# Attention and a routed expert layer on one core: the order of the loads at the start of the kernel

## The chip, the core and the metric

The kernel runs on one core of one Trainium2 chip. The metric is the device time of one execution in microseconds (us); less is better. TensorE multiplies matrices and transposes, VectorE (DVE) and ScalarE (ACT) work on rows, GpSimd (POOL) does some of the element work and the indirect transfers, and SyncE (SP) issues nearly all other transfers. Every engine runs its own instructions in order, so an instruction that waits holds back all that stand behind it on its engine; this goes for SP's transfers too.

## What is computed

Causal attention over a window of 128 positions with a slope per head, and then a layer of 8 experts, of which each token takes the one with the largest gate logit:

```
batch, n_heads, seq, head_dim = (8, 8, 576, 64)
scores = scale * np.matmul(q, k.transpose(0, 1, 3, 2))
bias = slopes[:, None, None] * (-np.abs(rel).astype(np.float32))[None, :, :]
mask = (rel >= 0) & (rel < window)
scores = np.where(mask, scores + bias[None], -1000000000.0)
attn = np.exp(scores - max) / (sum + 1e-09);  x = attn @ v
logits = x @ w_gate;  expert_idx = np.argmax(logits, axis=1)
out[token] = gate_w[token] * np.maximum(x[token] @ w1[e], 0.0) @ w2[e]
```

All inputs are float32.

## The kernel before

**Attention** goes over the 8 batches in pairs. 576 rows of a batch are 4 blocks of 128 queries and a rest of 64, and the rests of two batches make one block together, so there are 36 chunks of 128 query rows (`make_chunks`); chunk 4 is the first such pair of rests (batches 0 and 1), chunk 5 the first block of batch 1. A chunk looks at no more than 256 keys: chunk m of a batch needs the key columns from 128(m-1) to 128(m+1). The 8 heads lie in 4 pairs, and a pair fills the 128 partitions with twice 64 values.

A chunk's work is cut into operations with letters, once for each half of the heads where there is a digit: S (bias matmuls from a table, then query times key), F (fold the window and take the row maximum on DVE), E (exponentials on ACT), T (transposes on TensorE), C (copy to `pT` on ACT), P (masks on POOL), A (probabilities times values), X (copy on ACT), R (matmul with `iw_sb`, which holds an identity and the gate weights), L and Y (scaling on DVE, then the write of the rows to DRAM by SP).

**What sets the order.** Attention is recorded in steps (`step(s)`), four to a chunk, and within `tc.manual_schedule` the instructions of every engine stand in just that order up to step 152. The table `WHEN` gives each operation its time in chunks after the chunk's start: S0 of chunk c stands in step 4c, F1 at 0.604, A0 at 2.75 (so A of chunk 0 in step 11, A of chunk 1 in step 15), R at 4.027 (R of chunk 0 in step 16). Loads stand in steps too: `ahead` puts a query block at QA = -16 steps, its scaling on POOL at ZA = -6 and the values at VA = +1 step from the chunk's start.

**The start.** Ahead of step 0 stand, on SP: the first 128 key columns of batch 0 (L62), the table `cb_sb` with the bias in two halves of columns (L117; the first half serves the first two pairs of heads), the masks `c1_sb` (L118), then query block 1, key columns 128 to 320, the constants `c2_sb` (L425; its first 128 columns are the identity of the transposes), query block 2, key columns 320 to 576, value block 0 (L80), `iw_sb` (L133) and value block 1. Query block 0 is issued by ACT. Meanwhile TensorE does 8 matmuls on zeros (L104 and L98) and DVE scales query block 0 (L75). The loads that follow (query blocks 3 and the two rests, the keys of batch 1 by pairs of heads at L67) come out of `ahead` at step 0 and later. Transfers take eight semaphores in turn, so each one waits until the eighth before it has landed.

The weights of the experts' narrow tiles (`w_n`, 1 MB, L847) belong to the later part of the kernel and aren't in the manual order: a scheduler puts each of their loads at a free place on SP.

**The experts** follow: tokens are gathered by expert, and two layers of matmuls with weights split in a high and a low part fill TensorE to the end.

Of the kernel before, what the change touches and what calls it, by code (L numbers as in the profile page):

```python
# [10 lines left out]
F32 = mybir.dt.float32  # L11
# [4 lines left out]
ALU = mybir.AluOpType  # L16
# [16 lines left out]
def keep(tc, ins):  # L33
    return ins if HELD[0] else tc.keep_in_program_order(ins)


def attention(ctx, tc, st, qT, kT, v, c1, cb, iw, load_c2, logits, chunk_done, chunks, begun):
    nc = tc.nc
    const = ctx.enter_context(tc.tile_pool(name="a_const", bufs=1))
    qkv = ctx.enter_context(tc.tile_pool(name="a_qkv", bufs=2))  # L40
# [10 lines left out]
    batch = {}  # L51
    blocks = {}
# [3 lines left out]
        turns.append(turns.pop(0))  # L56
        return turns[-1]

    def load_k(c, d):
        if c == 0:  # L60
            batch[0] = qkv.tile([128, NP, S], F32, name="k_sb", bufs=2)
        nc.sync.dma_start(out=batch[0][:, :, c:d], in_=kT[0][:, :, c:d])  # L62

    def load_pair(b, p):
        if p == 0:
            batch[b] = qkv.tile([128, NP, S], F32, name="k_sb", bufs=2)
        nc.sync.dma_start(out=batch[b][:, p], in_=kT[b][:, p])  # L67

    def load_q(b, m, eng=nc.sync):
        blocks["q", b, m] = q = qkv.tile([128, NP, 128], F32, name="q_sb", bufs=QBUF)  # L70
        eng.dma_start(out=q, in_=qT[b, m])

    def scale_q(eng, b, m):
        q = blocks["q", b, m][:, :, 0:128 if m < 4 else S - 512]
        eng.tensor_scalar(out=q, in0=q, scalar1=0.125, scalar2=1.0, op0=ALU.mult, op1=ALU.mult)  # L75

    def load_v(b, m):
        n = min(128, S - 128 * m)
        blocks["v", b, m] = x = qkv.tile([128, DM], F32, name="v_sb", bufs=VBUF)
        nc.sync.dma_start(out=x[0:n], in_=v[b, 128 * m:128 * m + n])  # L80
# [6 lines left out]
    iw_sb = const.tile([128, NP, XW], F32, name="iw_sb")  # L87
# [23 lines left out]
        bank = score_banks()[:, 0] if op not in "zog" else None  # L111
        st["early"][0](op, bank if bank is None else bank.rearrange("p a b -> p (a b)"))

    load_k(0, 128)
    load_q(0, 0, nc.scalar)
    for c, d in ((0, 576), (576, cb.shape[1])):
        nc.sync.dma_start(out=cb_sb[:, c:d], in_=cb[:, c:d])  # L117
    nc.sync.dma_start(out=c1_sb, in_=c1)  # L118
    first = const.tile([128, 1], F32, name="first")
    nc.vector.memset(first, 0.0)  # L120
# [2 lines left out]
    warm_up(WU[0] - 4)  # L123
    st["warm"] = lambda k: (list(map(early, LE[k])), warm_up(LW[k]))

    scale_q(nc.vector, 0, 0)
    load_q(0, 1)
    load_k(128, 320)
    load_c2()
    load_q(0, 2)  # L130
    load_k(320, S)
    load_v(0, 0)
    nc.sync.dma_start(out=iw_sb, in_=iw)  # L133
    load_v(0, 1)

    def is_tail(subs):
        return subs[0][0] != subs[2][0]
# [95 lines left out]
            in1=rinv.rearrange("q (p c) -> q p c", c=2).unsqueeze(3).to_broadcast([128, NP, 2, n]), op=ALU.mult)  # L233

    ahead = {}
    seen = {("q", 0, 0), ("q", 0, 1), ("q", 0, 2), ("v", 0, 0), ("v", 0, 1), ("z", 0, 0)}
    first = {0}
    for ch, subs in enumerate(chunks):
        for b, m in dict.fromkeys((b, i // 4) for b, i in subs):
            want = [("q", b, m, load_q, QA), ("z", b, m, lambda b, m: scale_q(nc.gpsimd, b, m), ZA),  # L240
                    ("v", b, m, load_v, VA)]
            if m == 4:
                want.append(("v", b, 3, load_v, VA))
            for kind, b, j, f, at in want:
                if (kind, b, j) not in seen:
                    seen.add((kind, b, j))
                    ahead.setdefault(max(0, 4 * ch + at + SHIFT.get((kind, b % 2, j), 0)), []).append((f, b, j))
        for b in {b for b, _ in subs} - first:
            first.add(b)
            for p in range(NP):  # L250
                ahead.setdefault(4 * ch + KA + KD * p, []).append((load_pair, b, p))
    plan = []
    for ch, subs in enumerate(chunks):
        at = {**WHEN[None], **WHEN.get(ch, {})}
# [49 lines left out]
    def step(s):  # L304
        st["step"] = s
        if s == 0:
            begun(0)
        if s == 12:
            begun(1)
        for f, b, m in ahead.get(s, ()):  # L310
            f(b, m)
        while plan and plan[0][0] < (s + 1) / 4 - 1e-6:
            _, _, op, ch = plan.pop(0)
            do(op, ch)
        if s < len(WU) - 1:
# [24 lines left out]
    s = HAND  # L340
# [77 lines left out]
def load_consts(tc, st, c2):  # L418
    nc = tc.nc
    c2_sb = st["r_const"].tile(list(c2.shape), F32, name="c2_sb")  # L420
    o = 0
    for n, w in CONSTS:
        st[n] = c2_sb[:, o:o + w]
        o += w
    return lambda: nc.sync.dma_start(out=c2_sb, in_=c2)  # L425


def moe_setup(ctx, tc, st):
# [16 lines left out]
    st["base"] = base  # L445
    st["idx"] = const.tile([128, E * TT], U32, name="idx")

# [588 lines left out]

def layouts(q, k, v):
    heads = lambda a: a.reshape(B, NP, 2, S, D).transpose(0, 2, 4, 1, 3).reshape(B, 128, NP, S)
    qp = np.zeros((B, 128, NP, 640), q.dtype)
    qp[..., 0:S] = heads(q)  # L1040
    qT = np.ascontiguousarray(qp.reshape(B, 128, NP, 5, 128).transpose(0, 3, 1, 2, 4))
# [11 lines left out]
    return dict(qT=qT, kT=np.ascontiguousarray(heads(k)), v=vv, c1=c1,  # L1053
                cb=cb.reshape(128, -1).astype(ml_dtypes.bfloat16))


# [136 lines left out]


@with_exitstack
def attn_moe_kernel(ctx, tc, qT, kT, v, c1, cb, c2, iw, w12, out):
    nc = tc.nc
    st = {"stages": []}
    moe_pools(ctx, tc, st)
    load_c2 = load_consts(tc, st, c2)  # L1200
    moe_early(ctx, tc, st)
    weight_stream(ctx, tc, st, w12)
    chunks = make_chunks()
    lgs = {}

    with ExitStack() as actx:
# [46 lines left out]
        attention(actx, tc, st, qT, kT, v, c1, cb, iw, load_c2, logits, done, chunks, begun)  # L1253
# [45 lines left out]
```

## Time and profile before

| | us |
|---|---|
| median of 3 runs | 646.49 (645.24 to 649.17) |
| the profiled execution's own time | 648.7 |
| its span in the trace | 646.6 |
| TensorE busy in the span | 632.9 (98%) |
| granted TensorE clock, mean | 0.996 of full |

The profile is of one execution. The span begins 2.1 us or so after what the time counts; a time inside the trace is us from the span's start. A busy share is an average over the whole: what the start costs is read from the first 30 us, in the chain of waits (which piece of work released the next), in the timeline of each engine, and in tables of busy time by stretch, which also give the clock that TensorE was granted.

### The profile page before, as it was taken

What the parts mean: (1) busy time and instruction counts of PE and PEld (TensorE: products, weight loads), DVE (VectorE), ACT (ScalarE), POOL (GpSimd) and SP (SyncE); (2) the same over time, 40 slices, a digit from 0 to 9 for tenths busy, and PEclk for the clock granted to TensorE, in tenths of its full rate; (3) what the DMA queues carried; (4) which work ended last, traced back from release to release, by engine and by line L of the source; (5) the groups of instructions that cost most, each with busy time, mean ns of one, the idle gap of its engine ahead of it and who ended that gap; (6) DMA issues with size and microseconds to landing.
All of it is one profiled execution on the core that took longest, in us unless ns stands there. A gap on an engine that the chain in (4) does not pass through costs nothing.

```text
span 646.6 us, 17910 instructions
## 1 busy us (share of the span) xinstructions
PE 632.9 (98%) x7125; PEld 540.0 (84%) x7125; DVE 382.4 (59%) x940; ACT 318.2 (49%) x963; POOL 294.8 (46%) x405
## 2 busy tenths in 40 slices
PE   7999999999999999999999999999999999999996
PEld 3788888878887988988989899898898888888884
DVE  3458878869888786545543654555455456355411
ACT  5778888889877314533342334334233333333311
POOL 2644648668645040076227606733760750570202
PEclk9899999999999999999999999999999999999999
DMA  8765888777734152473535325434543532544101
GB/s 287 249 204 155 267 262 236 233 255 221 220 105 117 51 172 77 161 251 105 188 109 172 107 75 180 120 90 130 154 108 97 176 120 77 180 118 134 66 1 61
DMA packets 47288, 98.49 MB, mean 152 GB/s; under 512 B 12053, under 2 KB 14101, under 8 KB 47202
## 3 DMA queue, kind: packets, MB, share of 16 engines
q1 hardware_dynamic: 38722, 77.30, 37.8%
q0 software_dynamic: 8336, 19.76, 10.5%
q8 instruction: 57, 0.93, 0.6%
q10 hardware_dynamic: 144, 0.26, 0.1%
q14 instruction: 29, 0.24, 0.1%
HBM read 78.32 MB, written 18.98 MB: 150 GB/s over the span
## 4 chain that ended last, share of the span: by engine, by line
PE 74%; issue 10%; DVE 7%; POOL 4%; ACT 3%; DMA 1%; POOLq 0%; SPq 0%; ACTq 0%; DVEq 0%
PE y_ps L898 25%; PE l_ps L702 24%; PE b_ps L218 7%; PE s_ps L160 5%; PE b_ps L187 4%; PE r_ps L226 4%; POOL xg L682 2%; PE s_ps L151 2%; ACT pe L179 2%; DVE nmax L173 2%; DVE s_ps L170 1%; POOL out L886 1%; PE x_ps L663 1%; DMA cb_sb<-cb 1%; PE y_ps L858 1%
## 5 line engine op out<-in xcount | busy, mean ns | idle before, releaser
L705 ACT ACTIVATE hh<-l_ps 128x336 fp32r<-128x336 f32 (+7 forms) x104 | 46.5, 448 | 203.6 <-PE l_ps L702 203.3
L709 DVE SCALAR_TENSOR_TENSOR hl<-l_ps,hh 128x336 fp32r<-128x336 f32 (+7 forms) x104 | 52.0, 501 | 151.0 <-ACT hh L705 150.8
L682 POOL DMA_INDIRECT xg<-xd,od_idx x112 | 116.5, 1040 | 34.8 <-issue 33.8
L179 ACT ACTIVATE pe<-s_ps,nmax 128x128 f32<-128x128 f32 x288 | 105.5, 383 | 31.5 <-DVE nmax L173 24.7
L898 PE MATMUL y_ps<-wh,hh 128*128 128x512 f32 (+5 forms) x280 | 110.8, 396 | 0.0
L898 PE MATMUL y_ps<-wh,hl 128*128 128x512 f32 (+5 forms) x280 | 110.4, 394 | 0.0
L898 PE MATMUL y_ps<-wl,hh 128*128 128x512 f32 (+5 forms) x280 | 110.2, 394 | 0.0
L886 POOL DMA_INDIRECT out<-y,od_pidx x33 | 34.8, 1056 | 151.7 <-ACT y L904 145.5
L202 POOL TENSOR_SCALAR_AFFINE_SELECT pT<-pT 128x512 f32<-128x512 f32 x112 | 72.1, 652 | 66.4 <-ACT pT L282 65.0
L990 DVE TENSOR_TENSOR wl<-w_raw,wh 128x512 fp32r<-128x512 f32 x114 | 73.9, 690 | 32.0 <-ACT wh L986 30.6
L702 PE MATMUL l_ps<-xh,wh 128*128 128x304 f32 (+9 forms) x416 | 81.7, 318 | 0.0
L702 PE MATMUL l_ps<-xh,wl 128*128 128x304 f32 (+9 forms) x416 | 81.0, 316 | 0.0
L702 PE MATMUL l_ps<-xl,wh 128*128 128x304 f32 (+9 forms) x416 | 80.8, 316 | 0.0
L702 PEld LDWEIGHTS l_ps<-xh,wh 128*128 128x128 f32 x416 | 68.0, 189 | 8.4 <-issue 1.2
L702 PEld LDWEIGHTS l_ps<-xh,wl 128*128 128x128 f32 x416 | 66.3, 189 | 1.9
L702 PEld LDWEIGHTS l_ps<-xl,wh 128*128 128x128 f32 x416 | 66.3, 189 | 1.7
L218 PE MATMUL b_ps<-pT,v_sb 128*64 128x128 f32 (+2 forms) x1152 | 66.1, 265 | 0.1
L218 PEld LDWEIGHTS b_ps<-pT,v_sb 128*64 128x64 f32 (+1 forms) x1152 | 57.0, 136 | 9.3 <-issue 5.1
L898 PEld LDWEIGHTS y_ps<-wh,hl 128*128 128x128 f32 (+5 forms) x280 | 51.4, 183 | 13.6
L179 ACT ACTIVATION_READ_ACCUMULATOR pe<-s_ps,nmax 128x1 f32 x288 | 62.6, 218 | 0.0
L986 ACT CAST wh<-w_raw 128x1024 fp32r<-128x1024 f32 x57 | 59.5, 1044 | 4.6 <-DMA w_raw<-w 4.6
L898 PEld LDWEIGHTS y_ps<-wl,hh 128*128 128x128 f32 (+5 forms) x280 | 51.5, 184 | 11.4
(214 smaller groups left out, 923.1 us busy)
## 6 DMA issues: line engine op xcount, KB each, us to landing
w_raw<-w SPq DMA_DIRECT2D x64, 512.0 KB, 3.7
q_sb<-qT SPq DMA_DIRECT2D x39, 256.0 KB, 4.8
xd<-x_sb SPq DMA_DIRECT2D x32, 258.0 KB, 3.4
v_sb<-v SPq DMA_DIRECT2D x32, 256.0 KB, 4.2
k_sb<-kT SPq DMA_DIRECT2D x28, 288.0 KB, 4.8
w_n<-w SPq DMA_DIRECT2D x4, 1024.0 KB, 5.6
xg<-xd,od_idx POOLq DMA_INDIRECT x112, 3.2
xd<-x_sb SPq DMA_DIRECT2D x8, 129.0 KB, 2.7
```

What stands on the lines that cost most here:

```text
L160: nc.tensor.matmul(out=s_ps[rows(u), c, n, x0:x1], lhsT=blocks["q", b, m][h, 2 * g + n, rows(u % 2 if tail else u)], rhs=batch[b][h, 2 * g ...
L179: nc.scalar.activation(out=pe[:, h, :], in_=s_ps[:, c, n, lo:lo + 128], func=AF.Exp, bias=nmax[:, 2 * c + n:2 * c + n + 1], scale=1.0, acc ...
L202: nc.gpsimd.affine_select(out=part(cut(kb)), in_=part(cut(1)), pattern=pat(sign), base=0, channel_multiplier=-sign, compare_op=op, fill=0.0)
L218: nc.tensor.matmul(out=x_ps[64 * c:64 * c + 64, p, q], lhsT=blocks["v", b, m - 1 + kb][0:kk, D * h:D * h + D], rhs=pT[0:kk, kb, h, q], sta ...
L682: ins = tc.nc.gpsimd.indirect_dma_start(out=g[:, s], out_offset=None, in_=parts, in_offset=bass.IndirectOffsetOnAxis(ap=idx[:, s], axis=0),)
L702: nc.tensor.matmul(out=ps, lhsT=a[:, 128 * d:128 * d + 128], rhs=b[:, d], start=(k == 0), stop=(k == 11))
L705: nc.scalar.activation(out=hh, in_=ps, func=AF.Relu)
L709: nc.vector.scalar_tensor_tensor(out=hl, in0=ps, scalar=0.0, in1=hh.bitcast(F32), op0=ALU.max, op1=ALU.subtract)
L886: ins = nc.gpsimd.indirect_dma_start(**kw).ins
L898: nc.tensor.matmul(out=ys[t][0:n], lhsT=a[:, tl], rhs=b[:, 512:1024], start=(f == 0 and k == 0), stop=(f == 7 and k == 2))
L986: keep(tc, nc.scalar.copy(out=wh, in_=raw))
L990: keep(tc, eng.tensor_tensor(out=wl[:, sl], in0=raw[:, sl], in1=wh.bitcast(F32)[:, sl], op=ALU.subtract))
```

## The change

The first loads come in another order, in other pieces, and spread over the first 21 steps.

- Ahead of step 0, ACT issues query block 0 in two halves (by pairs of heads) and SP the table's halves and the first 128 key columns' halves in turn, then the masks, query block 1, key columns 128 to 256 and only the first 128 columns of the constants.
- The others stand in a table by step (`opening`). Where `gate` is set, a fill (`hold`, a DVE memset of one column of the tile that the load will overwrite) stands ahead of the load, so that SP can't issue it before DVE has come to that place.
- Keys come in four pieces of columns for all pairs of heads (`KEYS`), for every batch, instead of by pairs.
- The rest of 64 queries comes from an array of its own (`qE`), 128 KB instead of a padded 256 KB.

```diff
-    load_k(0, 128)
-    load_q(0, 0, nc.scalar)
-    for c, d in ((0, 576), (576, cb.shape[1])):
+    batch[0] = qkv.tile([128, NP, S], F32, name="k_sb", bufs=2)
+    q0 = qkv.tile([128, NP * 128], F32, name="q_sb", bufs=QBUF).rearrange("p (n x) -> p n x", n=NP)
+    blocks["q", 0, 0] = q0
+    for p, c, d in ((0, 0, 576), (2, 576, cb.shape[1])):
+        nc.scalar.dma_start(out=q0[:, p:p + 2], in_=qT[0, 0, :, p:p + 2])
         nc.sync.dma_start(out=cb_sb[:, c:d], in_=cb[:, c:d])
+        nc.sync.dma_start(out=batch[0][:, p:p + 2, 0:128], in_=kT[0, :, p:p + 2, 0:128])
     nc.sync.dma_start(out=c1_sb, in_=c1)
...
-    scale_q(nc.vector, 0, 0)
+    for p in (0, 2):
+        nc.vector.tensor_scalar(out=q0[:, p:p + 2], in0=q0[:, p:p + 2], scalar1=0.125, scalar2=1.0, op0=ALU.mult, op1=ALU.mult)
     load_q(0, 1)
-    load_k(128, 320)
-    load_c2()
-    load_q(0, 2)
-    load_k(320, S)
-    load_v(0, 0)
-    nc.sync.dma_start(out=iw_sb, in_=iw)
-    load_v(0, 1)
+    load_k(0, 1)
+    load_c2(0, 128)
...
+    opening = {1: [lambda: load_q(0, 2, True), lambda: load_k(0, 2)], 5: [lambda: load_q(0, 3, True), lambda: load_k(0, 3)],
+               7: [lambda: load_q(0, 4, True), lambda: load_q(1, 4), lambda: load_v(0, 0)],
+               9: [lambda: load_c2(128, None), lambda: load_k(1, 0, True)], 11: [lambda: load_q(1, 0, True), lambda: load_v(0, 1)],
+               13: [lambda: load_k(1, 1, True)], 15: [lambda: load_q(1, 1, True), load_iw],
+               17: [lambda: load_k(1, 2)], 21: [lambda: load_k(1, 3)]}
...
+    def hold(x):
+        keep(tc, nc.vector.memset(x, 0.0))
...
+KEYS = ((0, 128), (128, 256), (256, 384), (384, S))
```

The order on SP from the program's start, before (L62 keys, L71 queries, L80 values, L425 constants, L133 `iw_sb`):

```order
L62 DMA k_sb_117<-kT 128x4x128
L117 DMA cb_sb_107<-cb 128x576
L117 DMA cb_sb_107<-cb 128x512
L118 DMA c1_sb_106<-c1 128x256
L71 DMA q_sb_137<-qT 128x512
L62 DMA k_sb_117<-kT 128x4x192
L425 DMA c2_sb_64<-c2 128x389
L71 DMA q_sb_141<-qT 128x512 [waits DMAHW0_49]
L62 DMA k_sb_117<-kT 128x4x256 [waits DMAHW1_49]
L80 DMA v_sb_144<-v 128x512 [waits DMAHW2_49]
L133 DMA iw_sb_108<-iw 128x576 [waits DMAHW3_49]
```

The same place on SP in the changed program (L129 and L66 keys, L80 queries, L445 constants, L867 the narrow tiles' weights):

```order
L128 DMA cb_sb_107<-cb 128x576
L129 DMA k_sb_117<-kT 128x2x128
L128 DMA cb_sb_107<-cb 128x512
L129 DMA k_sb_117<-kT 128x2x128
L130 DMA c1_sb_106<-c1 128x256
L80 DMA q_sb_140<-qT 128x512
L66 DMA k_sb_117<-kT 128x4x128 [waits DMAHW0_49]
L445 DMA c2_sb_64<-c2 128x128 [waits DMAHW1_49]
L867 DMA w_n_5257<-w12 128x4x512 [waits DMAHW2_49]
L80 DMA q_sb_213<-qT 128x512 [waits DMAHW3_49,DVE_49]
L66 DMA k_sb_117<-kT 128x4x128 [waits DMAHW4_49]
L80 DMA q_sb_294<-qT 128x512 [waits DMAHW5_49,DVE_49]
```

The table now stands first, query block 2 (`q_sb_213`) and the third piece of keys behind it wait for DVE, and the 1 MB load of `w_n`, which stood behind 24 other transfers, has moved into the ninth place, ahead of both.

On DVE, from the second fold of chunk 3 (`nmax_522`) to R of chunk 0 (`r_ps_579`), before:

```order
L294 RECIPROCAL rinv_482<-rsum_227 128x8
L170 COPY_PREDICATED s1_ps_105<-c1_sb_106,s1_ps_105 128x4x128
L173 TENSOR_REDUCE nmax_522<-s1_ps_105 128x4
L170 COPY_PREDICATED s0_ps_104<-c1_sb_106,s0_ps_104 128x4x64
L173 TENSOR_REDUCE nmax_593<-s0_ps_104 128x4
```

The same place on DVE in the changed program (L187 and L190 are the fold, L69 the fill; `q_sb_532` is block 1 of batch 1):

```order
L311 RECIPROCAL rinv_486<-rsum_218 128x8
L69 MEMSET k_sb_392 128x1
L187 COPY_PREDICATED s1_ps_105<-c1_sb_106,s1_ps_105 128x4x128
L190 TENSOR_REDUCE nmax_528<-s1_ps_105 128x4
L69 MEMSET q_sb_532 128x1
L187 COPY_PREDICATED s0_ps_104<-c1_sb_106,s0_ps_104 128x4x64
```

And on SP there (L145 is `iw_sb`, L1252 the write of the first chunk's rows):

```order
L66 DMA k_sb_392<-kT 128x4x128 [waits DMAHW0_49,DVE_49]
L89 DMA v_sb_514<-v 128x512 [waits DMAHW1_49]
L80 DMA q_sb_532<-qT 128x512 [waits DVE_49,DMAHW2_49,PE_49,Pool_49]
L145 DMA iw_sb_108<-iw 128x576 [waits DMAHW3_49]
L80 DMA q_sb_556<-qT 128x512 [waits DMAHW4_49,PE_49,Pool_49]
L1252 DMA xd_63<-x_sb0_113 128x516 [waits DMAHW5_49,DVE_49]
```

The load of `iw_sb` stood eleventh on SP; it now stands right behind a query load that waits for a fill, and that fill stands behind the second fold of chunk 3.

## Rows read from the trace of the kernel before

**Rows 1.** The page, part 1: busy us (share) xinstructions.

```profile
PE 632.9 (98%) x7125; PEld 540.0 (84%) x7125; DVE 382.4 (59%) x940; ACT 318.2 (49%) x963; POOL 294.8 (46%) x405
```

**Rows 2.** Stretches: us, busy (x) by engine, clock, DMA share, GB/s.

```profile
10.00:20.00 10.00, 7.50 (x157) 4.38 (x142) 5.71 (x10) 7.06 (x33) 3.43 (x7) 0.83 1.06 387
12.43:16.39 3.96, 1.51 (x45) 1.01 (x44) 2.18 (x4) 2.85 (x15) 0.51 (x1) 1.00 1.06 388
16.39:19.80 3.41, 3.41 (x47) 1.79 (x46) 1.50 (x4) 2.30 (x10) 2.30 (x6) 0.50 1.05 381
19.80:60.00 40.20, 40.06 (x971) 33.21 (x971) 24.42 (x55) 33.88 (x144) 22.44 (x42) 1.00 0.68 205
120.00:160.00 40.00, 39.25 (x939) 33.07 (x937) 32.79 (x79) 35.44 (x146) 30.64 (x48) 1.00 0.80 248
```

**Rows 3.** Chain that ended last: start us, us, what.

```profile
1.54 4.05 DMA cb_sb<-cb
...
7.68 1.52 ACT pe L179 x8
...
14.79 1.44 issue
16.23 0.37 PE b_ps L187
16.60 0.40 PE s_ps L151 x8
17.00 1.07 PE s_ps L160 x30
...
22.86 0.26 PE s_ps L151 x8
...
23.67 1.90 PE b_ps L218 x32
25.57 0.26 PE s_ps L151 x8
...
26.96 0.98 PE r_ps L226 x8
```

**Rows 4.** Timeline: start us, us, engine, line, operation [idle before].

```profile
1.13 0.06 DVE L120 MEMSET first<- 128x1 f32 x1
2.92 1.91 PE L104 MATMUL b_ps<-warm 128*128 128x512 bf16 x4
5.38 0.55 SPq L62 DMA_DIRECT2D k_sb<-kT  x1
13.58 0.74 PE L160 MATMUL s_ps<-k_sb,q_sb 64*32 64x160 f32 x32
24.60 0.69 DVE L173 TENSOR_REDUCE nmax<-s_ps 128x4 f32<-128x512 f32 x1
```

**Rows 5.** Queues in 13.6 to 14.8 us: packets, MB, share of 16 engines.

```profile
q8 instruction: 1, 0.02, 5.8%
```

**Rows 6.** Transfers issued in 0 to 10 us: KB each, us to landing.

```profile
k_sb<-kT SPq DMA_DIRECT2D x1, 512.0 KB, 6.6
k_sb<-kT SPq DMA_DIRECT2D x1, 256.0 KB, 3.4
q_sb<-qT ACTq DMA_DIRECT2D x1, 256.0 KB, 2.6
```

**Rows 7.** Transfers issued in 34.7 to 37.3 us.

```profile
v_sb<-v SPq DMA_DIRECT2D x1, 256.0 KB, 3.6
```

**Rows 8.** Transfers issued in 16.5 to 19.5 us.

```profile
v_sb<-v SPq DMA_DIRECT2D x1, 256.0 KB, 5.3
```

**Rows 9.** PE's timeline near 133 us.

```profile
133.13 0.28 PE L151 MATMUL s_ps<-cb_sb 64*32 64x256 bf16 x2 [0.66 <-issue]
```

More of the change, by code (lines that the diff above doesn't have):

```diff
@@ L34, in keep, with attention @@
     return ins if HELD[0] else tc.keep_in_program_order(ins)
-def attention(ctx, tc, st, qT, kT, v, c1, cb, iw, load_c2, logits, chunk_done, chunks, begun):
+def attention(ctx, tc, st, qT, qE, kT, v, c1, cb, iw, load_c2, logits, chunk_done, chunks, begun):
     nc = tc.nc
@@ L57, in score_banks, with load_k, load_q @@
         return turns[-1]
[L59 to L65, printed above, removed]
-            batch[b] = qkv.tile([128, NP, S], F32, name="k_sb", bufs=2)
[L67 to L71, printed above, removed]
+    def load_k(b, i, gate=False):
+        if b not in batch:
+            batch[b] = qkv.tile([128, NP, S], F32, name="k_sb", bufs=2)
+        c, d = KEYS[(i - b % 2) % 4]
+        x = batch[b][:, :, c:d]
+        if gate:
+            hold(x[:, 0, 0:1])
+        nc.sync.dma_start(out=x, in_=kT[b][:, :, c:d])
+    def hold(x):
+        keep(tc, nc.vector.memset(x, 0.0))
+    def load_q(b, m, gate=False):
+        q = qkv.tile([128, NP * 128], F32, name="q_sb", bufs=QBUF)
+        q = q.rearrange("p (n x) -> p n x", n=NP) if m < 4 else q[:, 0:64 * NP].rearrange("p (n x) -> p n x", n=NP)
+        blocks["q", b, m] = q
+        if gate:
+            hold(q[:, 0, 0:1])
+        if m == 4:
+            nc.sync.dma_start(out=q, in_=qE[b])
+        else:
+            nc.sync.dma_start(out=q, in_=qT[b, m])
     def scale_q(eng, b, m):
-        q = blocks["q", b, m][:, :, 0:128 if m < 4 else S - 512]
+        q = blocks["q", b, m]
         eng.tensor_scalar(out=q, in0=q, scalar1=0.125, scalar2=1.0, op0=ALU.mult, op1=ALU.mult)
@@ L124, in attention, with load_iw @@
     st["warm"] = lambda k: (list(map(early, LE[k])), warm_up(LW[k]))
-    scale_q(nc.vector, 0, 0)
+    for p in (0, 2):
+        nc.vector.tensor_scalar(out=q0[:, p:p + 2], in0=q0[:, p:p + 2], scalar1=0.125, scalar2=1.0, op0=ALU.mult, op1=ALU.mult)
     load_q(0, 1)
-    load_k(128, 320)
-    load_c2()
-    load_q(0, 2)
-    load_k(320, S)
-    load_v(0, 0)
-    nc.sync.dma_start(out=iw_sb, in_=iw)
-    load_v(0, 1)
+    load_k(0, 1)
+    load_c2(0, 128)
+    def load_iw():
+        nc.sync.dma_start(out=iw_sb, in_=iw)
+    opening = {1: [lambda: load_q(0, 2, True), lambda: load_k(0, 2)], 5: [lambda: load_q(0, 3, True), lambda: load_k(0, 3)],
[3 more added lines that the diff above has]
+               17: [lambda: load_k(1, 2)], 21: [lambda: load_k(1, 3)]}
     def is_tail(subs):
@@ L235, in attention @@
     ahead = {}
-    seen = {("q", 0, 0), ("q", 0, 1), ("q", 0, 2), ("v", 0, 0), ("v", 0, 1), ("z", 0, 0)}
-    first = {0}
+    seen = {("q", 0, m) for m in range(5)} | {("q", 1, m) for m in (4, 0, 1)} | {("v", 0, 0), ("v", 0, 1), ("z", 0, 0)}
+    first = {0, 1}
     for ch, subs in enumerate(chunks):
@@ L250, in attention @@
             for p in range(NP):
-                ahead.setdefault(4 * ch + KA + KD * p, []).append((load_pair, b, p))
+                ahead.setdefault(4 * ch + KA + KD * p, []).append((load_k, b, p))
     plan = []
@@ L309, in step @@
             begun(1)
+        for f in opening.get(s, ()):
+            f()
         for f, b, m in ahead.get(s, ()):
@@ L424, in load_consts @@
         o += w
-    return lambda: nc.sync.dma_start(out=c2_sb, in_=c2)
+    return lambda c, d: nc.sync.dma_start(out=c2_sb[:, c:d], in_=c2[:, c:d])
 def moe_setup(ctx, tc, st):
@@ L1038, in layouts @@
     heads = lambda a: a.reshape(B, NP, 2, S, D).transpose(0, 2, 4, 1, 3).reshape(B, 128, NP, S)
-    qp = np.zeros((B, 128, NP, 640), q.dtype)
-    qp[..., 0:S] = heads(q)
-    qT = np.ascontiguousarray(qp.reshape(B, 128, NP, 5, 128).transpose(0, 3, 1, 2, 4))
+    qh = heads(q)
+    qT = np.ascontiguousarray(qh[..., 0:512].reshape(B, 128, NP, 4, 128).transpose(0, 3, 1, 2, 4))
+    qE = np.ascontiguousarray(qh[..., 512:])
     vv = np.ascontiguousarray(v.transpose(0, 2, 1, 3).reshape(B, S, DM))
@@ L1052, in layouts @@
             cb[c, :, 64 + 256 * p:320 + 256 * p] = np.where(back < 0, -1.0e9, slope * back)
-    return dict(qT=qT, kT=np.ascontiguousarray(heads(k)), v=vv, c1=c1,
+    return dict(qT=qT, qE=qE, kT=np.ascontiguousarray(heads(k)), v=vv, c1=c1,
                 cb=cb.reshape(128, -1).astype(ml_dtypes.bfloat16))
@@ L1195, in attn_moe_kernel @@
 @with_exitstack
-def attn_moe_kernel(ctx, tc, qT, kT, v, c1, cb, c2, iw, w12, out):
+def attn_moe_kernel(ctx, tc, qT, qE, kT, v, c1, cb, c2, iw, w12, out):
     nc = tc.nc
@@ L1251, in done @@
                     st["stages"].append([r, st["step"] + (c0 not in PACE), c0])
-        attention(actx, tc, st, qT, kT, v, c1, cb, iw, load_c2, logits, done, chunks, begun)
+        attention(actx, tc, st, qT, qE, kT, v, c1, cb, iw, load_c2, logits, done, chunks, begun)
     st["rc"] = ctx.enter_context(tc.tile_pool(name="rc", bufs=1))
```

## The prediction, made before the changed kernel ran

> **What bounds the kernel now.** I read the page's busy times first, then the table by stretches, the chain of waits, and the engines' timelines around its gaps. TensorE (PE) is busy for 632.9 of 646.6 us [rows 1], and from 19.8 us on it has hardly a hole: 40.06 of 40.20 us [rows 2]. So nothing in the opening matters but when PE gets to its full stretch, and a wait put on PE after 20 us is paid in full. The reader is to see three losses ahead of 20 us. The first scores start when the table lands, 4.05 us after its issue at 1.54 [rows 3], at 5.63, though the warm-up matmuls are through at 2.92 + 1.91 = 4.83 [rows 4]: 0.8 us. In the middle of four transposes PE stops at 14.79 for 1.44 us with "issue" as the reason: no tile was missing [rows 3]. And from 16.39 to 19.80 the granted clock is 0.50, that is 1.2 instead of 2.4 GHz, after a stretch in which PE had been busy for 1.51 of 3.96 us [rows 2]; 3.41 us at half speed cost 1.7 us. That makes 3.9 us in all, of which the change could win most and not more; 1% of the time, about what a measurement of this kernel can tell from no change, is 6.5 us.
>
> In the stop at 14.79 the only packet of the queue called instruction is under way: one of 0.02 MB in 13.6 to 14.8 us [rows 5]. I read it as PE waiting for its own instructions, while the transfers run at 387 GB/s from 10 to 20 us, which is all they reach [rows 2].
>
> **The change, part by part** (times inside the trace of before, 648.7 us by its own time, 2.2 above the median of 646.49).
>
> *First scores.* They need the table's first half (144 KB) and the first halves of query block 0 and of the keys (128 KB each): 400 KB. Before, 512 KB had landed at 0.78 + 3.4 = 4.2 us [rows 6]. So the data is there by 4.2; at worst the table takes its 4.05 us from 0.8 on, 4.85. Either way the warm-up's end at 4.83 decides: start 4.87, gain 0.75. The chain behind it (fold, exponentials of 1.52 us [rows 3], scores of chunk 1) is a chain of latencies and moves along: query block 1 has 1168 KB up to its end as before, and the keys 1424 instead of 1552.
>
> *Third chunk.* Its queries and keys now stand behind `w_n`, which moved from the 25th to the ninth place on SP. Up to the end of these keys 3024 KB are asked for, against 2514 before, and those landed at 5.38 + 6.6 = 12.0 [rows 4, 6]. The 510 KB more (0.52 MB) take 1.35 us at 387 GB/s [rows 2]: 13.3. Before, the products began at 13.58 [rows 4]. So of the lead of 0.75 here only 0.25 is left.
>
> *The stop for instructions.* PE comes to the same place at 14.55. If the packet stands in line behind the data, 3024 KB had been asked for by the time that PE asked, against some 3800 before; 0.8 MB less is 2.1 us at 387 GB/s, more than the 1.44. Bounds: the stop stays whole (0), or goes (-1.44). I take that it goes: lead 0.25 + 1.44 = 1.7.
>
> *The clock.* Without the stop PE runs on. Bounds: the clock falls as before (0), or not (-1.7). The stretch with 1.51 of 3.96 us busy [rows 2] has no like without the stop, so I take -1.7: lead 3.4. ACT's exponentials of chunk 2 and the copy of x between them are then as late as PE, which leaves about 3.0 at the end of the second scores of chunk 3: 20.7 instead of 23.67 [rows 3].
>
> *The values.* Block 0 ends at 4176 KB asked for: 1661 KB (1.70 MB) behind the 2514, so 12.0 + 4.4 = 16.4, while A of chunk 0 is due some 2 us after 14.55: the stretch of 3.41 us at half clock held the same scores, transposes and warm-ups. That costs nothing, or some 0.3. Block 1 waits for the fill behind the second fold of chunk 2 and comes up to 0.8 late for A of chunk 1; the next wait covers this.
>
> *The gate weights.* This is the term that decides. The load of `iw_sb` stands on SP behind a query load, which waits for the fill behind the second fold of chunk 3. In the trace the scores of that fold end at 23.67, its maximum at 24.60 + 0.69 = 25.29, and PE is at R of chunk 0 at 26.96 [rows 3, 4]. So the fold ends 1.62 after the scores, R is due 3.29 after them, and 1.67 lie between. In these must now go: the fill, 0.06 [rows 4], the issue of the query load, 0.55 at most [rows 4], and `iw_sb`'s own way. Before, it was issued ahead of 7 us and nobody waited. A load behind another of its size in a calm stretch takes 3.6 us from issue to landing [rows 7]; the ends are 2.6, the shortest of the start [rows 6], and 5.3 [rows 8]. With 3.6 it lands 0.06 + 0.5 + 3.6 = 4.15 after the fold: 20.7 + 1.62 + 4.15 = 26.5, and PE, there at 24.0, waits 2.5 us. R starts 0.5 earlier than before, not 3.0. With 2.6 it is 1.5 earlier, with 5.3 it is 1.2 later. No engine covers this: PE is in order, and behind R stand the transposes and scores of chunks 3 and 4.
>
> *The clock again.* A wait of 2.5 us leaves PE busy for some 1.5 of the 3.96 us ahead of 26.5, like the row before the fall [rows 2]. Ends: no fall (0), or 3.41 us at half speed (+1.7). By the nearest row I take +1.7.
>
> *The rest.* The other six fills, 0.06 us each, lie in DVE's idle time. Keys by columns come no later than by pairs, since only the piece in use must be there. The half-sized rests save 128 KB a batch that nobody waits for. I cost these at nothing; if their cover goes, the fourth rival has the price.
>
> Sum at R of chunk 0: -0.5 + 1.7 = +1.2 us, 649.9 by the profiled execution's own time and 647.7 by the median. Behind it PE is full, so this stays to the end.
>
> **Rivals.**
> *The wait is short* (0.30). `iw_sb` lands within 2.6 us or PE comes later by itself, and the clock holds: between the whole lead of 3.0, 643.5, and 0.5, 646.0; I put it at 644.7. For it speaks that the queue is nearly empty by then, against it the 3.6 of a pair of loads [rows 7].
>
> *The ring stays full* (0.17), so the spacing doesn't do what it says. `w_n` early keeps the transfers at 387 GB/s until some 17 us, the stop at 14.55 stays, and the clock falls there and again at R. Second scores of chunk 3 end at 23.67 - 0.25 = 23.4, R is at 23.4 + 1.62 + 4.15 = 29.2, 2.2 late, and with 1.7 for the clock it is +3.9: 650.4. For it speaks that PE has short stops of the same kind, 0.66 us near 133, where the transfers' engines are busy for 0.80 and not full [rows 2, 9], so the line of data alone may not set the packet's time. The Trainium skill says, in DMA: Bandwidth & Descriptors, section Queues, rings and completion order, that an engine takes turns between the queue rows at packets, so that an instruction packet would wait for a few packets of SP's and not for its whole line. By that rule the 1.44 us would not go with the line's length; the term of the stop would be 0, and the sum some 1.4 higher. When the packet was asked for no row here shows, so the trace can't settle it.
>
> *Slower, by the pieces of keys* (0.08). From batch 2 on a piece is 512-byte rows instead of 2304. The transfers' engines are busy for 0.80 at 120 to 160 us, and PE already stops there once for 0.66 [rows 2, 9]. If the smaller rows cost each of the six batches one such stop, that is 4.0 on top of 1.2: 651.7. It decides from the point where "issue" ends PE's idle time in 60 to 200 us once per batch.
>
> **How the numbers follow.** My forecast has 0.45: 647.7, with 646 to 649.5 for the landing of `iw_sb` and the clock. The short wait lies below it (0.30), the full ring and the pieces above (0.17, 0.08). Leaving out the lower third of the first and the ends of the last two gives 643.7 to 651.3. Over 1% faster means under 640.0, beyond all of the 3.9 that there is to win: 0.03. Over 1% slower means above 653.0, the ends of the last two rivals together: 0.06. Within 1%: 0.91.
>
> **What would show it.** In the profile after: first scores at 4.9; third chunk's products near 13.3, held by a load; no "issue" stop of over 0.3 us near 14.5 and no stretch at 0.50 before 20 us; then R of chunk 0 near 26.5 behind a wait of 2 to 3 us that the landing of `iw_sb` ends, and a granted clock of 0.50 after it. If R doesn't wait for `iw_sb`, the main term is wrong; if the stop near 14.5 stays with the ring emptier, its reading is.

## The result and the profile after

| | before | after |
|---|---|---|
| median of 15 runs each, us | 646.16 (643.24 to 649.17) | 652.12 (647.49 to 653.87) |
| the profiled execution's own time, us | 648.70 | 652.94 |
| span of its trace, us | 646.6 | 651.1 |
| granted clock, mean of that execution | 0.996 | 0.992 |

The change makes the kernel slower: ratio 1.0089, 95% interval 1.0073 to 1.0105, that is 5.8 us [4.7 to 6.8]. The forecast was 647.7 with a range up to 651.3; the measured time lies above it. Two slow runs of the kernels below, one of b1 at 3463.09 us and one of e10 at 776.77, are left out of their ratios and mean clocks.

TensorE's busy time hardly moved (632.9 in [rows 1]); what grew is the span with its holes:

```profile
PE 633.0 (97%) x7125; PEld 540.2 (83%) x7125; DVE 382.0 (59%) x948; ACT 317.9 (49%) x963; POOL 294.1 (45%) x405
```

The stretches of the start, with the columns of [rows 2] (us, busy by engine, clock, DMA share, GB/s):

```profile
10.00:14.21 4.21, 1.47 (x37) 0.72 (x17) 1.92 (x5) 3.54 (x18) 0.62 (x1) 1.00 1.02 311
12.43:14.21 1.78, 0.00 (x2) 0.03 (x1) 0.00 (x0) 1.50 (x9) 0.62 (x1) 1.00 1.00 322
15.47:18.88 3.41, 3.39 (x47) 1.79 (x46) 2.66 (x8) 2.50 (x10) 2.24 (x6) 0.50 0.52 157
26.50:28.82 2.32, 0.01 (x2) 0.01 (x1) 0.84 (x3) 1.50 (x7) 1.27 (x2) 1.00 0.89 340
29.13:32.54 3.41, 3.41 (x44) 2.87 (x50) 0.82 (x2) 0.81 (x3) 0.15 (x1) 0.50 0.02 5
120.00:160.00 40.00, 37.76 (x909) 31.43 (x907) 30.89 (x76) 33.43 (x135) 28.54 (x44) 1.00 0.77 225
```

The reader is to see two waits in which PE does nothing (1.78 and 2.32 us), a stretch of 3.41 us at clock 0.50 (1.2 GHz) soon behind each, and 2.2 us of idle time at 120 to 160, where before had 0.75 [rows 2]. The chain of waits names what ended the two:

```profile
4.83 0.34 PE s_ps L168 x8
...
6.88 7.20 DMA k_sb<-kT
14.08 0.14 issue
14.21 0.78 PE s_ps L177 x32
...
22.10 0.65 PE s_ps L177 x32
...
24.27 0.04 DVE q_sb L69
...
24.45 0.33 SPq L80
24.78 0.05 issue
24.83 3.94 DMA iw_sb<-iw
28.77 0.04 issue
28.82 2.03 PE r_ps L243 x8
```

Against [rows 3]: the first scores start at 4.83, not 5.63. The third chunk's products wait for key columns 256 to 384 and start at 14.21, not 13.58. The stop of 1.44 in the middle of the transposes is gone. The second scores of chunk 3 end at 22.75, not 23.67. R of chunk 0 waits for the gate weights and starts at 28.82, not 26.96. The issues on SP (start, us to issue) show what stands ahead of those keys:

```profile
5.23 0.44 SPq L867 DMA_DIRECT2D w_n<-w  x1
6.50 0.34 SPq L80 DMA_DIRECT2D q_sb<-qT  x1
6.88 0.60 SPq L66 DMA_DIRECT2D k_sb<-kT  x1
```

From R on PE is 3.2 us behind the first trace of before at the same matmul. It is 4.0 behind at 50 us, after a short stop with "issue" as the reason at 47 us, and 4.4 from 160 us to the end.

### The profile page after: what moved, and what is told of

Same layout as the page of the kernel before. It is cut to its first block, busy times and chain, and to the rows that moved or that the text cites. A ratio compares the mean times of both kernels' runs of the same rounds, so it can differ in the third digit from the quotient of the medians.

```text
span 651.1 us, 17932 instructions
## 1 busy us (share of the span) xinstructions
PE 633.0 (97%) x7125; PEld 540.2 (83%) x7125; DVE 382.0 (59%) x948; ACT 317.9 (49%) x963; POOL 294.1 (45%) x405
## 4 chain that ended last, share of the span: by engine, by line
PE 76%; issue 10%; DVE 5%; POOL 4%; DMA 2%; ACT 2%; POOLq 0%; SPq 0%; ACTq 0%; DVEq 0%
PE y_ps L918 25%; PE l_ps L722 24%; PE b_ps L235 7%; PE s_ps L177 5%; PE b_ps L204 5%; PE r_ps L243 4%; POOL xg L702 2%; PE s_ps L168 2%; DVE nmax L190 1%; ACT pe L196 1%; POOL out L906 1%; DMA k_sb<-kT 1%; DVE s_ps L187 1%; PE x_ps L683 1%; DMA iw_sb<-iw 1%
## 5 line engine op out<-in xcount | busy, mean ns | idle before, releaser
L918 PEld LDWEIGHTS y_ps<-wh,hl 128*128 128x128 f32 (+5 forms) x280 | 51.4, 183 | 13.6
```

The source lines that it names most:

```text
L918: nc.tensor.matmul(out=ys[t][0:n], lhsT=a[:, tl], rhs=b[:, 512:1024], start=(f == 0 and k == 0), stop=(f == 7 and k == 2))
```

## The experiments

The experiments ran on three chips, each beside runs of the kernel before, whose median there was 648.6 to 649.75; only ratios to those runs are compared. The clock in the last column is the mean over a kernel's runs of their granted clock. Before's 0.9966 comes from the runs beside the experiments, since of those beside the change only one clock is on record. One more stretch of 3.41 us at 0.50 makes the mean of a run 0.0026 less (3.41 x 0.5 / 650). But the last 1.2 to 4.6 us of each trace, in which PE has no work left, are at 0.50 too; that moves a single run's mean by up to 0.0026 at no cost, so only means over many runs are read here. In the 15 runs of the change the four at 0.989 take 652.9 us on average and the two at 0.997 take 648.9: 0.5 us for 0.001. This is a rough price: fitted to the runs of e7 the same slope is 0.9, to those of e2 and e12 0.1.

| kernel | edit | ratio [95%] | mean clock |
|---|---|---|---|
| before | | 1 | 0.9966 |
| the change | | 1.0089 [1.0073, 1.0105] | 0.9923 |
| a0 | the change again | 1.0096 [1.0068, 1.0125] | 0.9933 |
| e1 | `w_n` late | 1.0123 [1.0091, 1.0154] | 0.9932 |
| e2 | gate weights early | 1.0029 [1.0009, 1.0048] | 0.9959 |
| e3 | e1 and e2 | 1.0042 [1.0021, 1.0064] | 0.9957 |
| b1 | before, gate weights late | 1.0039 [1.0018, 1.0060] | 0.9955 |
| e6 | e2, `w_n` at step 19 | 1.0047 [1.0020, 1.0074] | 0.9954 |
| e7 | e6 without fills | 1.0054 [1.0033, 1.0075] | 0.9949 |
| e8 | e6, values earlier | 1.0001 [0.9979, 1.0023] | 0.9928 (0.9970 without one run at 0.946) |
| e9 | e8, `w_n` at step 15 | 0.9995 [0.9974, 1.0016] | 0.9973 |
| e10 | the change, later keys by pairs | 1.0067 [1.0040, 1.0094] | 0.9934 |
| e11 | e9 and e10 | 0.9991 [0.9967, 1.0015] | 0.9975 |
| e12 | e2 and e10 | 1.0020 [1.0004, 1.0037] | 0.9948 |
| b2 | before, first loads alone | 0.9994 [0.9972, 1.0016] | 0.9966 |

**e2, the gate weights at step 9** in place of step 15:

```diff
-               9: [lambda: load_c2(128, None), lambda: load_k(1, 0, True)], ...
+               9: [lambda: load_c2(128, None), load_iw, lambda: load_k(1, 0, True)], ...
-               13: [lambda: load_k(1, 1, True)], 15: [lambda: load_q(1, 1, True), load_iw],
+               13: [lambda: load_k(1, 1, True)], 15: [lambda: load_q(1, 1, True)],
```

> The changed kernel, with the load of the gate weights and identity moved from step 15 to step 9, behind no fill but that of step 7. Theory: R of chunk 0 no longer waits (2.3 us) and the half-clock stretch of 3.4 us after it goes (1.7): 4 us less than the changed kernel, so 1 to 3 us over the kernel before. Rival (the wait only stands in for time that is lost to something else behind it): under 1.5 us less, near +4.5.

Measured 1.0029, as the theory had it: 3.9 us of the 5.8 are gone (0.0060 x 647; with both intervals, 2.2 to 5.5). In its chain R follows the matmuls ahead of it without a wait, while the keys still hold the third chunk:

```profile
7.06 7.72 DMA k_sb<-kT
14.78 0.14 issue
...
26.72 0.59 PE b_ps L204 x4
27.31 0.98 PE r_ps L243 x8
```

Its mean clock is 0.9959 against the change's 0.9923. At 0.5 us for 0.001 those 0.0036 are 1.8 us of the 3.9, an estimate, and the rest is the wait. Where in the kernel the time at half clock was saved is not shown. The profile of e2 has one half-clock stretch in the opening, behind the wait for keys, and the change's has two; but of the five profiles with a wait at R (the change 2.32 us, a0 1.39, b1 1.27, e10 2.84, e1 3.13) only the change's has such a stretch behind it. The stretch of e2, and R in e10, which runs on at full clock:

```profile
15.84:19.25 3.41, 3.08 (x49) 2.12 (x48) 2.38 (x5) 2.10 (x9) 2.48 (x6) 0.50 0.72 214
```

```profile
31.53 1.25 PE L248 MATMUL r_ps<-iw_sb,xT 128*128 128x144 f32 x8 [2.84 <-DMA iw_sb<-iw]
```

**b1, the gate weights late in the kernel before**, all else as before:

```diff
-    nc.sync.dma_start(out=iw_sb, in_=iw)
...
+        if s == 15:
+            keep(tc, nc.vector.memset(iw_sb[:, 0, 0:1], 0.0))
+            nc.sync.dma_start(out=iw_sb, in_=iw)
```

> The kernel before with one suspected cost alone: the load of the gate weights taken out of the opening and issued in step 15 behind a fill, with nothing else changed. Theory: R of chunk 0 waits 2 to 3 us for it, and a stretch at half clock follows: 2 to 4.5 us over the kernel before. Rival (a wait there is taken up by slack later): under 1 us.

Measured 1.0039, 2.5 us (1.2 to 3.9). The same one part makes the kernel before slower, and its trace has a wait at the same place. PE's own wait there is 1.27 us, not the 2 to 3 expected, and no half-clock stretch follows; but the profiled run, 650.42 us, is b1's shortest. The instruction stop ahead of it is still there:

```profile
14.52 1.32 issue
...
23.47 2.77 DMA iw_sb<-iw
26.24 0.14 issue
26.37 1.22 PE r_ps L225 x8
```

**e1, the load of `w_n` held to its place in program order**, which is late on SP, with **e3**, e1 and e2 together:

```diff
-        nc.sync.dma_start(out=w2s[p], ...)
+        ins = nc.sync.dma_start(out=w2s[p], ...)
+        if p == 0 and k == 0:
+            keep(tc, ins)
```

> The changed kernel, with the 1 MB load of the narrow tiles' weights moved from ninth on SP to behind attention. Theory (two waits of PE, each followed by a stretch at half clock): the last piece of keys for the third chunk lands near 11 us instead of 14.1, its products start near 12.8 instead of 14.2, the wait for the gate weights (2.3 us) stays. 1.4 to 3 us less than the changed kernel, so 3 to 4.5 us over the kernel before. Rival (the smaller key pieces of the later batches cost the time): no change from the changed kernel, near +5.8.

> The changed kernel with both moved: narrow weights behind attention, gate weights at step 9. Theory: both waits and both half-clock stretches go; the first scores still start 0.8 us earlier than before. From 2 us under the kernel before to 0.5 over it. Rival (key pieces, or the fills themselves): 2 us or more over the kernel before, with no gap of PE over 1 us ahead of 30 us.

Both missed, e1 by a wide margin (1.0123). The hold of the third chunk by its keys went, but PE, earlier now, stopped for values block 0 (2.13 us), whose load stands behind the fill of step 7, and in e1 again at R (3.13). And a cost came in that has nothing to do with the opening: where the experts start `w_n` is issued at 228.01, ahead of a write of the gate at 228.59 that the first gather needs. PE waits there for 1.95 us, the clock falls behind it, and against e2's trace e1 loses 3.3 us at this place and e3 3.5. So neither ratio is the price of `w_n` in the opening; e6 is the cleaner case. The two waits of e1's opening:

```profile
13.18 4.97 DMA v_sb<-v
18.15 0.14 issue
...
24.36 4.29 DMA iw_sb<-iw
28.64 0.04 issue
28.69 1.25 PE r_ps L243 x8
```

Each load of the opening is late by itself; taking one wait away shows the next.

**a0, the changed kernel again**, and three steps from e2: **e6** issues `w_n` in step 19, **e7** is e6 with the fills out, **e8** is e6 with values block 0 in step 1 and block 1 in step 9:

```diff
+               17: [lambda: load_k(1, 2)], 19: [lambda: st["first_narrow"]()], 21: ...
...
+    def first_narrow():
+        st["w_n"] = st["m_n"].tile([128, 4, DM], F32, name="w_n")
+        nc.sync.dma_start(out=st["w_n"], in_=w12[E][0:4, :, 512:1024].rearrange("f p c -> p f c"))
```

```diff
-        if gate:
-            hold(x[:, 0, 0:1])
...
-        if gate:
-            hold(q[:, 0, 0:1])
```

```diff
-    opening = {1: [lambda: load_q(0, 2, True), lambda: load_k(0, 2)], ...
+    opening = {1: [lambda: load_q(0, 2, True), lambda: load_k(0, 2), lambda: load_v(0, 0)], ...
-               7: [lambda: load_q(0, 4, True), lambda: load_q(1, 4), lambda: load_v(0, 0)],
+               7: [lambda: load_q(0, 4, True), lambda: load_q(1, 4)],
-               9: [lambda: load_c2(128, None), load_iw, lambda: load_k(1, 0, True)], 11: [lambda: load_q(1, 0, True), lambda: load_v(0, 1)],
+               9: [lambda: load_c2(128, None), lambda: load_v(0, 1), load_iw, lambda: load_k(1, 0, True)], 11: [lambda: load_q(1, 0, True)],
```

> The changed kernel itself, unaltered, timed with the next three on one chip. Theory and rival alike: 4 to 7 us over the kernel before, with the third chunk's products held by keys that stand behind the narrow weights and R of chunk 0 held by the gate weights.

> The changed kernel with the narrow weights' load written into step 19 and the gate weights into step 9. Theory: the third chunk starts near 13 us and nothing waits at R; what is left is value block 0, which stands behind the fill of step 7 and lands near 18, so that PE waits some 2 us near 16, as in the first run of this study. Between 1.5 us under the kernel before and 1.5 over it. Rival (key pieces of the later batches): 2 us or more over it.

> The run before this one without any fill: the loads of the opening stand in the same order on SP and wait for no place on DVE. Theory (the instruction packet stands in line behind the data): the transfers are at their full rate up to some 17 us, the packet starts near 11 to 13 us as in the kernel before instead of near 8, value block 0 is in time, and PE stops for instructions near 14.5, 0.3 to 1.4 us. Rival (the packet is late whatever the line): the packet starts at the same time with and without fills. Time within 1.5 us of the run with fills, either way.

> The run with narrow weights at step 19 and gate weights at step 9, fills kept, and value blocks 0 and 1 moved to steps 1 and 9. Theory: no wait for values and none for instructions, so no gap of PE over 1 us from 14 to 30 us, and 1 to 3 us under the kernel before. Rival (key pieces or fills cost the time): not under the kernel before.

a0 repeats the result. Its trace has no half-clock stretch in the opening, and R waits 1.39 us, since PE gets there at 26.17 and the weights at 27.52:

```profile
24.11 3.41 DMA iw_sb<-iw
27.52 0.04 issue
27.56 1.25 PE r_ps L243 x8
```

e6 (1.0047) missed its theory. It waits 1.91 us for values block 0 at 16.1, as was expected, and stops for 2.02 at 43.27, which was not; its profiled run is a long one, 657.37 against a median of 652.78. e7 felled my reading of the fills: without them the instruction packet starts at 9.75 us, with them (e6) at 9.69, and the time is the same, so the fills space nothing out that mattered. e7 has no wait for the values, is as far ahead as e8 until 39 us, and gives that back in stops with "issue" as the reason, of 1.03 us at 39.55, 1.33 at 128.96 and 1.04 at 140.70. e8 missed its theory too: it has no wait over 0.2 us between 16 and 39 us, is 4.1 us ahead of the first trace of before at 39 us, stops for 2.14 at 39.61 and ends level with before (1.0001).

**e9, `w_n` in step 15**, and **e10, e11, e12, the keys of batch 2 and later by pairs**, that is before's `load_pair` in the later loop:

```diff
-               13: [lambda: load_k(1, 1, True)], 15: [lambda: load_q(1, 1, True)],
-               17: [lambda: load_k(1, 2)], 19: [lambda: st["first_narrow"]()], 21: ...
+               13: [lambda: load_k(1, 1, True)], 15: [lambda: load_q(1, 1, True), lambda: st["first_narrow"]()],
+               17: [lambda: load_k(1, 2)], 21: ...
```

```diff
+    def load_pair(b, p):
+        if p == 0:
+            batch[b] = qkv.tile([128, NP, S], F32, name="k_sb", bufs=2)
+        nc.sync.dma_start(out=batch[b][:, p], in_=kT[b][:, p])
...
-                ahead.setdefault(4 * ch + KA + KD * p, []).append((load_k, b, p))
+                ahead.setdefault(4 * ch + KA + KD * p, []).append((load_pair, b, p))
```

> The e8 kernel (gate weights at step 9, values block 0 at step 1, values block 1 at step 9) with the expert weights w_n moved from step 19 to step 15, so that their 1 MB is issued at about 22 us, ahead of the first write of rows, where SP's line is nearly empty, and not at 28.5 us ahead of the keys of later blocks. Theory: the one large wait of e8 (PE 39.61 to 41.74, 2.1 us) came from those 1 MB; without it PE keeps e8's lead of 3.7 us over the kernel before to at least 100 us, and the time is 2 us under e8's: ratio 0.996 to 0.999 to the kernel before of the same call. Rival A: some other load behind the 1 MB is late instead (values or keys needed at 28 to 33 us), a wait of 1 us or more there, ratio 0.999 to 1.002. Rival B: what is won by 100 us is given back before the experts start at 215 us (as e7 gave back 3 us between 120 and 160 us), ratio 0.999 to 1.003.

> The changed kernel, with the keys of batch 2 and later by head pairs (2,304-byte rows) as in the kernel before, at the same steps; the opening is the changed one. It prices the fourth case of the prediction (column pieces with 512-byte rows cost waits when a batch starts). Theory: the pieces cost little; the waits of the changed kernel at 123, 135, 147 and 159 us (0.41, 0.78, 0.77, 0.29 in its trace) shrink by 1 us in all at most, and the ratio is 1.006 to 1.010 against the changed kernel's 1.009. Rival: the pieces cost 2 us or more, ratio 1.004 to 1.006.

> The e9 kernel with the keys of batch 2 and later by head pairs as in e10. If e9's lead of some 3.7 us meets waits at 120 to 160 us that come from the column pieces, this kernel is 1 us or more under e9 and its lead at 190 us is larger by as much. If the pieces are without effect it is within 0.5 us of e9.

> The changed kernel with both suspected costs out: the gate weights issued at step 9 (as e2, which measured 1.0029) and the keys of batch 2 and later by head pairs (as e10, 1.0067 against 1.0089 of the changed kernel). Expert weights and first loads as changed. Theory: the two add up, 1.0029 - 0.0022 = 1.0007, so 0.999 to 1.002, and what is left of the change costs and wins nothing that can be told. Rival A: the pieces cost nothing of their own and e10's difference was scatter: 1.002 to 1.004. Rival B: without the wait at R PE is further ahead and meets late instruction packets in 30 to 160 us, so that the two don't add up: 1.002 to 1.004 with idle time put down to issue of over 1.5 us in that stretch.

e9 came out at 0.9995, in the ranges of both rivals and above the theory's (0.996 to 0.999), which its interval still reaches. Its trace fells the theory's mechanism: the wait is not for keys behind `w_n`. PE stops after 27 of 32 products of one chunk, at the same instruction as in e8, with "issue" as the reason, and goes on 1.5 us after the one packet of the queue called instruction has passed (40.73 to 41.93). A like stop of 1.06 us stands at 36.29. The chain, and that queue in 40.7 to 42.0 us (packets, MB, share):

```profile
40.83 0.53 PE s_ps L177 x27
41.37 2.02 issue
43.38 0.74 PE s_ps L177 x4
```

```profile
q8 instruction: 1, 0.02, 5.7%
```

e11, whose later keys come in long rows, has the packet at 38.28 and stops for 0.37 at the same instruction. The change itself stops there for 0.31 us and a0 for 0.65. So this stop is of the kind of the one at 14.79, and what a quick opening wins is in part given back where PE has run ahead of its instructions. In e11:

```profile
39.98 0.53 PE s_ps L182 x27
40.51 0.37 issue
40.88 0.47 PE s_ps L182 x5
```

In time the pieces can't be told from nothing: e10 is 1.4 us under the change, e12 0.6 under e2, e11 0.3 under e9, each inside the intervals. e12 (1.0020) lies on the line between its theory and its first rival. The traces say more of the fourth rival, by which the pieces bring stops with "issue" as the reason at 60 to 200 us. The change has two of over 0.5 us there; e11, with the later keys by pairs, has them at the same places, and e2 and e9, with the keys in pieces, have neither. So they are not the pieces' doing. In e11:

```profile
129.33 0.28 PE L173 MATMUL s_ps<-cb_sb 64*32 64x256 bf16 x2 [0.76 <-issue]
140.50 1.18 PE L240 MATMUL b_ps<-pT,v_sb 128*64 128x64 f32 x28 [0.76 <-issue]
```

**b2, the first loads alone in the changed order**, in the kernel before (the queries' scaling goes by halves too):

```diff
-    load_k(0, 128)
-    load_q(0, 0, nc.scalar)
-    for c, d in ((0, 576), (576, cb.shape[1])):
+    for p, c, d in ((0, 0, 576), (2, 576, cb.shape[1])):
+        nc.scalar.dma_start(out=q0[:, p:p + 2], in_=qT[0, 0, :, p:p + 2])
         nc.sync.dma_start(out=cb_sb[:, c:d], in_=cb[:, c:d])
+        nc.sync.dma_start(out=batch[0][:, p:p + 2, 0:128], in_=kT[0, :, p:p + 2, 0:128])
```

> The kernel before with only the first loads in the changed order (first keys, queries and table by halves, queries on the other queue, scaled by halves); everything behind them as before. First scores start at 4.8 to 4.9 us, 0.75 earlier. Theory: PE then waits longer at 14 to 16 us, since the instruction packet's start hangs on the data ahead of it in line and not on PE, so that the lead is gone by 17 us: ratio 0.9995 to 1.0005. Rival: the lead stays, ratio 0.9985 to 0.9992.

Measured 0.9994, between the theory's range and the rival's, with both inside the interval. The first scores are 0.87 us earlier, but PE then waits 1.36 us for the keys of chunk 1, so that the lead is gone by 10 us and not, as the theory had it, at the packet. The packet starts at 13.56 as before (13.65), and PE still stops:

```profile
3.79 5.78 DMA k_sb<-kT
...
9.71 0.85 PE s_ps L164 x32
...
14.89 1.18 issue
```

**a1 and a2, the kernel before again** with no edit, two more profiles.

> The kernel before, unchanged, for a second profile of it. Theory: the half-clock stretch that its first profile shows at 16.39 to 19.80 us (1.7 us) is not there in each execution, as it is not in those of the two kernels built from it (gate weights late, first loads alone), though the same stop of 1.2 to 1.5 us near 14.5 us is. Then this profile's time is some 2 us under the first one's at the same place (matmul 500 at 27.4 to 28.0 us, not 29.41). Rival: the clock falls again in 15 to 20 us and matmul 500 is at 29.2 to 29.6.

> The kernel before, unchanged, for a third profile: as for the second. Together they say whether the 1.7 us that the prediction meant to win at the clock were there to be won in a usual execution.

The theory held in both: no half-clock stretch. The chain and the stretch 16.39 to 19.80 of a1, to be read against [rows 2, 3], with the stop at 1.00 and R at 25.57:

```profile
15.31 1.00 issue
...
25.57 0.98 PE r_ps L226 x8
```

```profile
16.39:19.80 3.41, 3.19 (x84) 2.34 (x92) 1.84 (x5) 3.12 (x15) 2.79 (x7) 1.00 1.06 386
120.00:160.00 40.00, 39.94 (x974) 33.54 (x974) 33.11 (x77) 35.02 (x142) 31.35 (x46) 1.00 0.77 249
```

and of a2, where R is at 25.81 and the stop is 0.40 in another place:

```profile
21.38 0.40 issue
...
25.81 0.98 PE r_ps L226 x8
```

Without the half-clock stretch, then, the kernel before has R 1.1 to 1.4 us earlier than the trace on which the sum was built. The profiles of b1 and b2, with stops of 1.32 and 1.18, have no such stretch in the opening either.

## Why the prediction was right and wrong

**First scores**: right, 4.83 for 4.87. b2 says what this is worth alone: nothing that can be told.

**Third chunk**: right in its cause, too small. The keys did stand behind `w_n`, and without it (e1) nothing holds these products; but they landed at 14.08, not 13.3. The transfers moved 311 GB/s from 10 us to there, not the 387 of before [rows 2] that I used.

**The stop for instructions**: right for this place. The packet starts at 11.85 and no stop follows. e1 differs from the change by the place of `w_n` alone and has PE within 0.1 us of it at the 72nd matmul, yet its packet starts at 7.82 us, 4.0 earlier. So the line of data has a part in the packet's time. The other runs with the changed opening agree, with some scatter: where `w_n` stands in it (the change, a0, e2, e10, e12) the packet starts at 10.65 to 13.00, where it doesn't at 7.82 to 10.65. By the rule of the Trainium skill that the prediction weighed (DMA: Bandwidth & Descriptors, Queues, rings and completion order), turns between the queue rows at packets, 1 MB less in SP's row would have moved it by little, if the packet is asked for at the same time in both; the trace doesn't agree with that. When the packet is asked for still no row shows.

**The clock**: this is the step that failed. "The stretch with 1.51 of 3.96 us busy [rows 2] has no like without the stop, so I take -1.7" was wrong twice. First, the stretch that I meant to win isn't in a usual execution of before: a1 has the stop, at 1.00 us, and no 0.50, and a2 has neither. The profiled execution was 2.2 us over the median, and I noted that without asking which of its rows made the 2.2. Second, in the profiled run of after the clock did fall, at 15.47, behind the wait for keys that took the stop's place. With those 1.7, and 0.9 that the third chunk lost beyond its forecast, the second scores of chunk 3 end at 22.75, for which I had 20.7: of the lead of 3.0 there 0.9 was left. To usual executions of before (a1, a2) there was no lead at all: they come to R at 25.57 and 25.81, PE in the change at 26.50.

**The gate weights**: the wait was right, 2.32 us for 2.5, and so was what ends it. What was wrong is where it starts. I had R at 26.5 because PE would be there at 24.0; but the load is issued behind a fill that DVE runs after the fold of chunk 3, and that fold runs as late as PE does (24.27, where I had 22.3). A late PE therefore doesn't shorten this wait, and the lateness and the wait add: R at 28.82, of which 2.05 us are the late scores and 0.35 a longer way from the fold's end to the landing (4.50 for 4.15). The issue to landing took 3.94, for which I had 3.6.

**The clock again**: it came true in the profiled run (29.13 to 32.54), where PE is 1.3 us further behind after it, for the 1.7 that I took. How far that was luck stays open: of five profiles with a wait at R, four, one of them with 3.13 us, have no such stretch behind it. Over the runs the mean clock is 0.9923 against 0.9966; at 0.5 us for 0.001 that is 2.2 us of the 5.8, an estimate from the spread of the change's own runs, which doesn't say where in the kernel they are.

**The rest**: "nothing" for the pieces is unsettled, between 0 and 1.5 us. The values cost nothing in the profiled run and 0.5 us in a0 for a bound of 0.3, since they land there at 17.58 and not at 16.4; where PE is not held by the keys (e1, e3, e6) they cost 1.9 to 2.1, so this term was small only because PE came late. "Behind it PE is full, so this stays to the end" was wrong: the lag grew from 3.2 us behind R to 4.4. At the stop at 47 us it grew by 0.8, at the second of the two stops below by 1.0, and by 0.2 behind them; 0.8 had been given back between. These two, 0.78 and 0.77 of the 2.2 us idle at 120 to 160 us, are "issue" with an instruction packet 1.4 us ahead of their ends (PE's timeline, idle time in brackets); a1 shows none there, e12 neither.

```profile
136.32 0.29 PE L168 MATMUL s_ps<-cb_sb 64*32 64x256 bf16 x3 [0.78 <-issue]
147.50 0.77 PE L235 MATMUL b_ps<-pT,v_sb 128*64 128x64 f32 x14 [0.77 <-issue]
```

**The sum after the fact**: from trace to trace the change is 4.2 us slower (652.94 less 648.70), of which the forecast had 1.2. Of the 3.0 between, 2.3 were there at R already (28.82 for 26.5) and 1.2 came by the later stops, while the second fall of the clock cost 0.4 less than its term. The medians are 6.0 apart, 1.7 more, since before's profiled run lay 2.5 over its median and the change's 0.8. By experiments, 5.8 us = 3.9 for the gate weights (the change less e2), 0.6 for the pieces, uncertain (e2 less e12), and 1.3 [0.3 to 2.4] that e12 keeps. In those 1.3 the hold of the third chunk, 2.21 us in e12's trace, with 6.83 us at half clock from 14.02 on, stands against the earlier first scores and the stop that is gone. Moving `w_n` out of the opening and the values up (e11) takes that away too, 0.9991. That e11 or b2 beats the kernel before is not shown; no kernel here does.

**The rivals.** "The ring stays full" gave R at 29.2 and +3.9; measured were 28.82 and +4.2 from trace to trace. Its numbers came true without its mechanism, which was the old stop staying: another wait, of 1.78 us, stood near the same place. The rival of a short wait is out. That of the pieces is out by its own sign, stops that come with the pieces; at most a part of the time is left for it.

## What to carry to other kernels

A load that is released by late work of the very engine it feeds (here by a fill behind DVE's fold of PE's scores) costs its way from issue to landing less the work that the engine has in between, however late that engine runs; here ways of 2.8 to 4.3 us made waits of 1.3 to 3.1. Count it as a constant, not as a slack that lateness eats. Before a forecast wins back a stretch that one trace shows, above all one at half clock, see in a second trace of the same kernel whether it is there, and ask what makes the profiled execution longer than the median. When a large load is pulled forward in a line that is kept in order, price the first load behind it that somebody waits for, and not the large one.

## What the runs showed of the chip that I had not expected

The instruction packet's start went with the data in line: 13.15 to 13.75 us in the three profiles of before, 11.85 and 11.77 with the change, 10.65 to 13.00 in e2, e10 and e12, 9.7 in e6, 7.82 in e1. PE went on some 1.4 us after the packet's end: at 16.23 after 14.77 in before, at 43.38 after 41.93 in e9, at 147.50 after 146.07 with the change, and in the other runs with such a stop between 1.27 (e8) and 1.51. The Trainium skill (Runtime: NRT & Kernel Launch, Instruction fetch mechanics) has an engine's instructions refilled in blocks of 16 KiB, with the fetch hidden behind the issue; the size agrees with the 0.02 MB of the packet's row, the hiding does not: the fetch cost 2.02 us in e9's chain.

The half-clock stretches differ between executions of one kernel on a chip: the 15 runs of the change have mean clocks from 0.989 to 0.997. The wait of 1.78 us in the change's profile was followed by one, a0's of 1.39 and e8's of 2.14 by none. In the first 50 us of all these profiles PE waits 13 times for 1.8 to 3.2 us; a stretch at 0.50 begins in or within 1.4 us behind eight of these waits (one of 3.22 in e10, one of 2.02 in e9), and behind the other five (one of 3.13 in e1) none does. Nor is a run's mean clock its time: one run of e8 at 0.946 took 652.31 us, 2.0 over that kernel's median.
